# One head's keys and values side by side: a regrouped pooling product in a fused attention, Fourier and feed-forward kernel

## The chip, the cores and the metric

The kernel runs on one core of a Trainium2 chip, in one launch. The metric is the device time of that launch in microseconds (us). A core has five engines that work side by side and hand over to each other by semaphores: TensorE (PE) multiplies matrices, VectorE (DVE), ScalarE (ACT) and GpSimd (POOL) do elementwise work, and SyncE (SP) issues the DMAs. PE takes a stationary matrix (a weight load, shown as PEld) and streams moving columns through it.

## The reference

For each of 8 batches and 8 heads, 576 tokens are pooled to 32 memory slots, and then every token attends to those slots. The result goes through a two-dimensional Fourier transform whose real part is added, a normalisation, and a feed-forward layer with a residual.

```python
a = exp(phi - max(phi));  a = a / (sum(a) + 1e-9)        # 576 x 32 per head
k_m = einsum('bhsm,bhsd->bhmd', a, k)                    # pooled keys,   32 x 64
v_m = einsum('bhsm,bhsd->bhmd', a, v)                    # pooled values, 32 x 64
attn = softmax(q @ k_m.T / sqrt(64));  x = attn @ v_m
u = x + real(fft(fft(x, axis=1), axis=2))
un = (u - mean(u)) / sqrt(var(u) + 1e-6)
out = u + relu(un @ w1) @ w2                             # 512 -> 2048 -> 512
```

## The kernel before, in words

Single-precision values are carried as two 16-bit parts, a high one and a low one, so that a product of two of them is three matmuls: high by high, low by high, high by low (low by low is dropped). The tokens of the feed-forward layer are cut into 18 chunks of 256. Each chunk goes through 8 units: in `ffn1_sums` 24 matmuls of 256 columns build a hidden tile `ph`, which ACT (L944) and DVE (L945) move out of PSUM as a high and a low part; in `ffn2` 12 matmuls of 512 columns accumulate into `po`. These two are most of what PE does.

The attention is written as a generator, `background()`, and the unit loop draws one step of it per unit. A scheduler that works at build time then interleaves everything and fixes the order on every engine; on the chip each engine runs its list in that order, and waits where an operand is not there yet.

The change is in `pair_memory`, for the batches from the third on (`b >= NX`, `NX = 2`): six batches of four pairs of heads, so 24 calls. A pair's keys and values arrive in one tile `kv` of 5 token tiles by 2 (`w` = 0 for keys, 1 for values) by 128 columns (two heads of 64). They are squared for a scale (L474, and L477 for the queries), scaled and cut into parts: the high part by ACT (L488), the low part of the keys by DVE (L495), the low part of the values by an ACT copy (L490) and a POOL subtraction (L491), because `KP = [1]`. The parts lie in `kvs`, the pooling weights of two pairs in `et`, also as high and low.

The pooling itself is two groups of 15 matmuls, first keys, then values, each of 64 moving columns (the 32 slots of both heads):

```python
for ka, kb in ((0, 0), (1, 0), (0, 1)):
    for t in range(NST):
        mm(pm[:, w * 64 : w * 64 + 64], lhsT=kvs[ka][:, t, w, :],
           rhs=et[:, g // 2, kb, t, 64 * (g % 2) : 64 * (g % 2) + 64], ...)
```

Half of what comes out, one head's keys with the other head's weights, is not wanted; the mask `mk` takes it away when DVE reads the keys (L516) and the values (L517) out of PSUM. The keys are then cut into parts (`km`, L526 on ACT and L527 on DVE) for `pair_scores`, whose 18 matmuls `psc` follow. At the end of a batch `values` multiplies the pooled values by a constant matrix that `load_vt` brings in (`pv`, L695), and `mix_x` uses them once more (`px`).

Of the kernel before, what the change touches and what calls it, by code (L numbers as in the profile page):

```python
# [10 lines left out]
F32 = mybir.dt.float32  # L11
F16 = mybir.dt.float16
BF16 = mybir.dt.bfloat16
# [3 lines left out]
AF = mybir.ActivationFunctionType  # L17
ALU = mybir.AluOpType
AX = mybir.AxisListType
PSUM = bass.MemoryType.PSUM  # L20

P = 128
B, H, S, D, M = 8, 8, 576, 64, 32
# [6 lines left out]
NST = 5  # L30
# [19 lines left out]
GATE2 = [[], ["un1", "qs0"]] + [["un1", f"ev{j - 2}"] for j in range(2, 8)]  # L50
NA = 2
NAH = 1
KP = [1]
BN = 2
UB = 2
NW = NF // UB
# [1 line left out]
EB = 14  # L58
# [80 lines left out]
def kernel(  # L139
# [10 lines left out]
    nc = tc.nc  # L150

    const = ctx.enter_context(tc.tile_pool(name="const", bufs=1))
# [9 lines left out]
    et = const.tile([P, 2, 2, NST, P], F16, name="et")  # L162
# [11 lines left out]
    small = const.tile([P, 832], F32, name="small")  # L174
    mk = small[:, 0:68]
    ones = small[:, 68:132].bitcast(BF16)
    qsb = [small[:, 196 + i * 258 : 196 + i * 258 + NJ] for i in range(2)]
    half = small[:, 712:713]
    drop = small[:, 715:716]
# [11 lines left out]
    stg = const.tile([P, 3, 4 * UW], F16, name="stg")  # L191
# [6 lines left out]
    hring = const.tile([P, NW, 2, 4, P], F16, name="hring")  # L198

    nk = 2 * NST * P  # L200
    kvs = [stg[:, 2, i * nk : (i + 1) * nk].rearrange("p (t w c) -> p t w c", t=NST, w=2) for i in range(2)]
    qs = [stg[:, 2, 2 * nk + i * NQ : 2 * nk + (i + 1) * NQ] for i in range(2)]
    et32 = et.rearrange("p g l t c -> p (g l t c)").bitcast(F32).rearrange("p (g t c) -> p g t c", g=2, t=NST)

# [28 lines left out]
    vmc = vmf.rearrange("p g u c -> p (g u c)")[:, : H * M]  # L233
# [2 lines left out]
    nc.gpsimd.memset(drop, 2.0**-14 - 0.5)  # L236
    for t in qsb:
        nc.gpsimd.memset(t, 0.0)
    scratch = const.tile([P, 400], F32, name="scratch")
    share = const.tile([P, 2 * NJ], F32, name="share")  # L240
    rings, taken = {}, [0]

    def tiny(tag, n, bufs=2):
        if tag not in rings:
            rings[tag] = [taken[0], 0]
            taken[0] += n * bufs
        o, i = rings[tag]
        rings[tag][1] += 1
        o += i % bufs * n
        assert taken[0] <= 400, taken  # L250
        return scratch[:, o : o + n]

    def high_words(t):
# [84 lines left out]
    def load_vt():  # L338

        v = stg[:, 1] if marks.get("vt") else hring.rearrange("p a l f c -> p (a l f c)")[:, : NG * 2 * DM]  # L340
        marks["vt"] = nc.sync.dma_start(out=v, in_=vt_d)
        return [v[:, g * 2 * DM : (g + 1) * 2 * DM] for g in range(NG)]

    def pooling_f32(b):
# [94 lines left out]
    def pair_memory(b, g, r, vmf, ivs):  # L439

        n = f"{b}_{g}"
        kv = r[:, :KV].rearrange("p (t w c) -> p t w c", t=NST, w=2)
        q = r[:, KV:]
        if b < NX:
            pm = psg.tile([P, 512], F32, tag="g", name=f"pm_{n}")
            mm = groups()
            busy = keep_busy(0, 0, f"pm_{n}") if b == 0 else None
            for w in range(2):
                for t in range(NST):
                    m = mm(  # L450
                        pm[:, w * 64 : w * 64 + 64],
                        lhsT=kv[:, t, w, :],
                        rhs=et32[:, g // 2, t, 64 * (g % 2) : 64 * (g % 2) + 64],
                        start=(t == 0),
                        stop=(t == NST - 1),
                    )
                    if b == 0:
                        keep_busy(1, 2 * P, n, busy, m)
            if b == 0 and g == 1:
                keep_busy(10, 2 * P, n, busy, m)  # L460
            kmf = share[:, g * 64 : g * 64 + 64] if b == 0 else tiny("kmf", 64, 2)
            mask = share[:, 256 + g * 64 : 320 + g * 64] if b == 0 else mk[:, 0:64]
            marks["kmf"] = marks[f"kmf{n}"] = nc.vector.tensor_tensor(out=kmf, in0=pm[:, 0:64], in1=mask, op=ALU.mult)
            nc.vector.tensor_tensor(
                out=vmf[:, g],
                in0=pm[:, 64:128].unsqueeze(1).to_broadcast([P, 2, 64]),
                in1=mask.unsqueeze(1).to_broadcast([P, 2, 64]),
                op=ALU.mult,
            )
            return q, None, kmf, 1.0 / 8.0  # L470
        am = tiny("am", 3, 1)
        with tc.issue_after(marks["wh3"].ins) if b == NX and g == 0 else nullcontext():
            for w in range(2):
                nc.scalar.activation(  # L474
                    kvs[0][:, :, w, :].bitcast(BF16), kv[:, :, w, :], AF.Square, accum_out=am[:, 1 + w : 2 + w]
                )
            nc.scalar.activation(  # L477
                kvs[1][:, 0:3].rearrange("p t w c -> p (t w c)").bitcast(BF16), q, AF.Square, accum_out=am[:, 0:1]
            )
        pm = psg.tile([P, 512], F32, tag="g", name=f"pm_{n}")  # L480
        mm = groups()
        mm(pm[:, 128:131], lhsT=ones, rhs=high_words(am), start=True, stop=True)
        sc = tiny("sc", 3, 2)
        isc = tiny("isc", 3, 2)
        norm_scale(sc, isc, pm[:, 128:131], 3, 14, n)
        nc.vector.tensor_copy(out=ivs[:, g : g + 1], in_=isc[:, 2:3])
        for w in range(2):
            nc.scalar.activation(kvs[0][:, :, w, :], kv[:, :, w, :], AF.Copy, scale=sc[:, 1 + w : 2 + w])  # L488
            if w in KP:
                nc.scalar.activation(kv[:, :, w, :], kv[:, :, w, :], AF.Copy, scale=sc[:, 1 + w : 2 + w])  # L490
                nc.gpsimd.tensor_tensor(  # L491
                    out=kvs[1][:, :, w, :], in0=kv[:, :, w, :], in1=kvs[0][:, :, w, :], op=ALU.subtract
                )
            else:
                nc.vector.scalar_tensor_tensor(  # L495
                    out=kvs[1][:, :, w, :],
                    in0=kv[:, :, w, :],
                    scalar=sc[:, 1 + w : 2 + w],
                    in1=kvs[0][:, :, w, :],
                    op0=ALU.mult,  # L500
                    op1=ALU.subtract,
                )
        for w in range(2):
            i = 0
            for ka, kb in ((0, 0), (1, 0), (0, 1)):
                for t in range(NST):
                    mm(
                        pm[:, w * 64 : w * 64 + 64],
                        lhsT=kvs[ka][:, t, w, :],
                        rhs=et[:, g // 2, kb, t, 64 * (g % 2) : 64 * (g % 2) + 64],  # L510
                        start=(i == 0),
                        stop=(i == 3 * NST - 1),
                    )
                    i += 1
        kmf = tiny("kmf", 64, 2)
        nc.vector.tensor_tensor(out=kmf, in0=pm[:, 0:64], in1=mk[:, 0:64], op=ALU.mult)  # L516
        nc.vector.scalar_tensor_tensor(  # L517
            out=vmc[:, g * 64 : g * 64 + 64],
            in0=pm[:, 64:128],
            scalar=isc[:, 2:3],  # L520
            in1=mk[:, 0:64],
            op0=ALU.mult,
            op1=ALU.mult,
        )
        km = tiny("km", 64).bitcast(F16).rearrange("p (l c) -> p l c", l=2)
        nc.scalar.copy(out=km[:, 0], in_=kmf)  # L526
        nc.vector.tensor_tensor(out=km[:, 1], in0=kmf, in1=km[:, 0], op=ALU.subtract)  # L527
        es = tiny("es", 1, 2)
        nc.vector.tensor_scalar(
            out=es, in0=isc[:, 0:1], scalar1=isc[:, 1:2], scalar2=1.0 / 8.0, op0=ALU.mult, op1=ALU.mult  # L530
        )
        return q, sc, km, es
# [215 lines left out]
    def mix_x(b, key, col, n, rows, attnT, vbd):  # L748
        px = psg.tile([P, 512], F32, tag="g", name=f"px_{b}_{key}")
        mm = groups()  # L750
        if b >= NX:
            for h in range(H):
                o = 64 * (h % 2)
                mm(
                    px[rows, h * 64 : h * 64 + 64],
                    lhsT=stack[h // 2][:, col // P * 2 + h % 2, col % P : col % P + n],
                    rhs=vbd[:, h, o : o + 64],
                    start=True,
                    stop=True,
                )  # L760
            return px
        vbd = vbd.rearrange("p (l g) f -> p l g f", l=2)
        for g in range(NG):
            for l in range(2):
                marks["px"] = mm(
                    px[rows, g * P : (g + 1) * P],
                    lhsT=attnT[:, g, col // P, col % P : col % P + n],
                    rhs=vbd[:, l, g, :],
                    start=(l == 0),
                    stop=(l == 1),  # L770
                )
        return px
# [457 lines left out]
    marks = {}  # L1230
# [106 lines left out]

    load_phi(0)
    nc.scalar.dma_start(out=mk, in_=mk_d)
    nc.scalar.activation(warm, warm, AF.Exp)  # L1340
    keep_busy(14, 2 * P, "start")
    parts_w1, parts_w2 = {}, {}
# [182 lines left out]
```

## Time and profile before

| | us |
|---|---|
| three runs | 938.22, 940.21, 937.79 |
| median | 938.22 |
| profiled execution, span from first to last instruction | 935.8 |
| PE busy | 925.7 (99%) |
| DVE busy | 635.4 (68%) |
| ACT busy | 498.2 (53%) |
| POOL busy | 222.3 (24%) |

The profile gives the span of the profiled execution; the time of a run holds also what lies around the span. A row of the lists by line reads: line, engine, operation, output <- inputs, shape, count, then the busy time in us and the mean length of one in ns, then the idle time of the engine just ahead of it. The lengths of matmuls overlap, since they are pipelined, so a run of them in the timeline, with its start, its length and its count, tells more than the mean. In the timeline a bracket at the end names an idle time before the row and what ended it.

### The profile page before, as it was taken

Reading aid. Unit: us, or ns where it says so; the run is one execution under the profiler, and the core shown is the slowest. Engines: PE = TensorE matmul, PEld = TensorE weight load, DVE = VectorE, ACT = ScalarE, POOL = GpSimd, SP = SyncE. Lnnn points to the kernel's source line nnn. Section 1 sums busy time; section 2 is a strip of 40 time slices with the busy share of each in tenths; the row PEclk is TensorE's granted clock in tenths of the full one; section 3 lists DMA queues with packets and bytes.
Section 4 is the critical chain, followed back from the end, with each engine's and each line's share of the span. In section 5 each row is a group of like instructions: output and inputs, shape, how many; then the busy total and the mean of one; then the engine's idle time right before and its main releaser. Section 6 shows DMA issues by size and latency. Waiting matters only on the chain.

```text
span 935.8 us, 19497 instructions
## 1 busy us (share of the span) xinstructions
PE 925.7 (99%) x7982; PEld 682.6 (73%) x7982; DVE 635.4 (68%) x1406; ACT 498.2 (53%) x980; POOL 222.3 (24%) x248
## 2 busy tenths in 40 slices
PE   8999999999999999999999999999999999999998
PEld 8776776667767677777767767777676777788886
DVE  4899786777677766667414876667555686985454
ACT  4678557765376536554414654655445543643331
POOL 3310142424133313323100331324120422100000
PEclk9999999999999999999999999999999999999999
DMA  9964651365246522844103541274215311202000
GB/s 353 368 233 135 206 143 14 83 146 118 50 88 141 118 49 56 169 88 108 22 25 69 142 115 49 38 191 108 38 46 97 97 27 37 46 23 47 1 23 23
DMA packets 131321, 92.04 MB, mean 98 GB/s; under 512 B 115744, under 2 KB 115744, under 8 KB 129184
## 3 DMA queue, kind: packets, MB, share of 16 engines
q1 hardware_dynamic: 131088, 90.77, 38.1%
q8 instruction: 62, 1.02, 0.5%
q14 instruction: 27, 0.22, 0.1%
q10 hardware_dynamic: 144, 0.03, 0.0%
HBM read 58.15 MB, written 9.44 MB: 72 GB/s over the span
## 4 chain that ended last, share of the span: by engine, by line
PE 82%; DVE 9%; ACT 4%; POOL 2%; issue 1%; DMA 0%; SPq 0%; DVEq 0%; ACTq 0%; POOLq 0%
PE ph L315 34%; PE po L954 29%; PE pm L315 3%; PE po L1044 3%; PE pq L1044 3%; PE psc L315 2%; PE pp_t L315 2%; PE po L913 1%; PE ph L891 1%; PE pa L726 1%; PE pv L695 1%; PE px_t L315 1%; DVE uring L825 1%; DVE w1t L1194 1%; DVE un L852 1%
## 5 line engine op out<-in xcount | busy, mean ns | idle before, releaser
L315 PE MATMUL ph<-unring,w1t 128*128 128x256 f16 x3264 | 388.8, 273 | 0.0
L315 PEld LDWEIGHTS <-w1t 128*128 128x128 f16 x3324 | 318.9, 98 | 58.4 <-issue 1.6
L954 PE MATMUL po<-w2s,hring 128*128 128x512 f16 x1368 | 319.8, 379 | 0.0
L954 PEld LDWEIGHTS <-hring 128*128 128x128 f16 x1368 | 130.8, 98 | 129.9 <-issue 0.5
L945 DVE SCALAR_TENSOR_TENSOR hring<-ph,hring 128x512 f16<-128x512 f32 x114 | 78.1, 685 | 52.4 <-ACT hring L944 51.9
L944 ACT ACTIVATE hring<-ph 128x512 f16<-128x512 f32 x114 | 67.0, 588 | 61.8 <-PE ph L315 61.3
L613 POOL TENSOR_TENSOR aring<-aring,scratch 128x384 f32<-128x384 f32 x30 | 26.8, 894 | 242.8 <-DVE scratch L611 197.3
L851 POOL TENSOR_TENSOR scratch<-scratch,small 128x1 f32<-128x1 f32 x36 | 22.4, 627 | 164.6 <-DVE scratch L848 160.8
L315 PEld LDWEIGHTS <-stg 128*128 128x128 f16 x1152 | 45.0, 98 | 10.7 <-issue 1.5
L550 ACT CAST aeo<-eo 128x384 f16<-128x384 f32 x30 | 15.3, 510 | 51.3 <-DVE eo L547 51.3
L605 ACT ACTIVATE aring<-aring,scratch 128x384 f32<-128x384 f32 x24 | 14.6, 609 | 46.9 <-DVE aring L602 46.9
L543 DVE TENSOR_TENSOR eo<-aring 128x128 f32<-128x128 f32 x29 | 35.4, 1221 | 4.9 <-POOL aring L630 4.9
L315 PE MATMUL pm<-et,stg 128*128 128x64 f16 (+1 forms) x780 | 37.0, 199 | 0.4 <-DMA et<-elt 0.4
L811 DVE SCALAR_TENSOR_TENSOR share<-pp_t,scratch,small 128x257 f32<-128x257 f32 (+1 forms) x48 | 21.1, 481 | 23.8 <-ACT small L807 22.4
L593 DVE TENSOR_REDUCE scratch<-psc 128x12 f32<-128x384 f32 x32 | 17.7, 554 | 27.7 <-PE pm L315 16.7
L630 POOL TENSOR_TENSOR aring<-aring 128x128 f32<-128x128 f32 x60 | 35.3, 608 | 2.3
L877 POOL TENSOR_TENSOR ud<-un,ud 128x1024 f16<-128x1024 f32 x13 | 27.6, 2126 | 30.8 <-ACT ud L876 30.8
L825 DVE SCALAR_TENSOR_TENSOR uring<-px_t,scratch,share 128x256 f32<-128x256 f32 (+1 forms) x80 | 34.2, 478 | 0.3 <-PE px_t L315 0.2
L491 POOL TENSOR_TENSOR stg<-rawt,stg 128x640 f16<-128x640 f32 x12 | 17.2, 1431 | 72.6 <-ACT rawt L490 72.6
L625 POOL TENSOR_TENSOR hring<-aring,hring 128x640 f16<-128x640 f32 x24 | 34.1, 1421 | 0.1
L1008 ACT ACTIVATE rawt<-ph 128x512 f32<-128x512 f32 x22 | 13.1, 596 | 35.0 <-PE ph L315 35.0
L891 PE MATMUL ph<-unring,w1t 128*128 128x256 f32 (+1 forms) x144 | 30.2, 358 | 0.7 <-ACT unring L863 0.7
(321 smaller groups left out, 1530.5 us busy)
## 6 DMA issues: line engine op xcount, KB each, us to landing
rawt<-in_raw SPq DMA_DIRECT2D x15, 640.0 KB, 4.8
stg<-in_raw SPq DMA_DIRECT2D x15, 640.0 KB, 5.3
out<-uring SPq DMA_DIRECT2D x36, 256.0 KB, 2.1
stg<-in_w SPq DMA_DIRECT2D x7, 1024.0 KB, 5.9
rawt<-in_raw SPq DMA_DIRECT2D x15, 384.0 KB, 3.3
stg<-in_raw SPq DMA_DIRECT2D x15, 384.0 KB, 3.1
phs<-in_raw SPq DMA_DIRECT2D x32, 160.0 KB, 5.3
w2s<-in_w SPq DMA_DIRECT2D x4, 1024.0 KB, 9.2
```

Of the source, the lines that this page charges most:

```text
L315: m = nc.tensor.matmul(out, lhsT=lhsT, rhs=rhs, start=start, stop=stop)
L543: nc.vector.tensor_tensor(out=eo[:, 0, 1:3], in0=ap[:, 1:3, 0], in1=ap[:, 1:3, 1], op=ALU.add)
L613: eng.tensor_tensor(out=a, in0=a, in1=sm.unsqueeze(2).to_broadcast([P, 12, M]), op=ALU.mult)
L625: nc.gpsimd.tensor_tensor(out=ahw[:, :, :, 1], in0=a10, in1=ahw[:, :, :, 0], op=ALU.subtract)
L630: eng.tensor_tensor(out=a2[:, i : i + 4], in0=a[:, 0:4], in1=a[:, 4:8], op=op)
L825: nc.vector.scalar_tensor_tensor(out=u[rows, hs], in0=px[rows, hs], scalar=igx[rows], in1=tm[rows, w * NJ + half : w * NJ + half + 256], o ...
L877: marks[f"ul{c}"] = (nc.vector if c in (1, LC, LC + 1, LC + 2) else nc.gpsimd).tensor_tensor(out=ud[:, 1], in0=un, in1=ud[:, 0], op=ALU.su ...
L891: marks[f"f1_{j}"] = nc.tensor.matmul(ph[:, cols], lhsT=w[:, k, f * P : (f + 1) * P], rhs=unTs[0][:, k, cols], start=(k == 0), stop=(k == ...
L944: marks[f"ev{c}_{j}"] = nc.scalar.activation(h[:, 0], phv, AF.Relu)
L945: nc.vector.scalar_tensor_tensor(out=h[:, 1], in0=phv, scalar=0.0, in1=h[:, 0], op0=ALU.max, op1=ALU.subtract)
L954: m = nc.tensor.matmul(po[t], lhsT=hs[j][:, lh, f * 2 + t], rhs=w2s[:, j * UB + f, lw, :], start=(j == 0 and f == 0 and i == 0), stop=(j = ...
L1044: m = nc.tensor.matmul(dst[:, half_n * 256 : half_n * 256 + 256], lhsT=a[:, la, f], rhs=b[:, f, lb], start=begin, stop=False, skip_group_c ...
```

## The change

Keys and values change places in the stationary matrix: instead of the keys of both heads, then the values of both heads, a matrix now holds one head's keys and the same head's values (64 + 64 columns). The moving columns are that head's 32 high weights and its 32 low weights together. So per head 5 matmuls of 64 columns do high by high and high by low at once, and 5 of 32 columns add low by high onto the first half; 20 matmuls in place of 30. The two halves of the result are then added by a new DVE reduction, and the keys and values are taken out of that sum (in SBUF, no longer in PSUM) with `mk` and its complement `mkv`, a new small tile that one POOL instruction makes near the start.

Two things follow from the layout. For the second head the columns stand as values, keys, so `parts_of` gives the keys the quarters 0 and 3 and the values 1 and 2; and the pooled values land on the other half of the partitions than before, so the second load of `load_vt` is done as two DMAs with the halves exchanged, and `mix_x` takes the other column offset. The parts of keys and values also exchange engines (`KP = [0]`): the low part of the keys is now made by ACT and POOL, that of the values by DVE.

```diff
-KP = [1]
+KP = [0]
...
-        marks["vt"] = nc.sync.dma_start(out=v, in_=vt_d)
+        halves = [slice(0, 64), slice(64, P)]
+        for dst, src in zip(halves, halves[::-1]) if marks.get("vt") else ((slice(0, P), slice(0, P)),):
+            load = nc.sync.dma_start(out=v[dst], in_=vt_d[src])
+        marks["vt"] = load
...
-            nc.scalar.activation(kvs[0][:, :, w, :], kv[:, :, w, :], AF.Copy, scale=sc[:, 1 + w : 2 + w])
+            src = kv[:, :, w, :].rearrange("p t (h c) -> p t h c", h=2)
+            hi, lo = (k[:, :, parts_of[w]] for k in kvs)
+            nc.scalar.activation(hi, src, AF.Copy, scale=sc[:, 1 + w : 2 + w])
...
-        for w in range(2):
-            i = 0
-            for ka, kb in ((0, 0), (1, 0), (0, 1)):
+        for h in range(2):
+            c0 = 64 * (g % 2) + 32 * h
+            heads = [k[:, :, 2 * h : 2 * h + 2].rearrange("p t x c -> p t (x c)") for k in kvs]
+            for t in range(NST):
+                both = mm(
+                    pm[:, h * 64 : h * 64 + 64],
+                    lhsT=heads[0][:, t],
+                    rhs=et[:, g // 2, :, t, c0 : c0 + M],
+                    start=(t == 0),
+                    stop=(t == NST - 1),
+                )
+            with tc.issue_after(both.ins):
                 for t in range(NST):
-                    mm(
-                        pm[:, w * 64 : w * 64 + 64],
...
+                    nc.tensor.matmul(
+                        pm[:, h * 64 : h * 64 + M],
+                        lhsT=heads[1][:, t],
+                        rhs=et[:, g // 2, 0, t, c0 : c0 + M],
+                        start=False,
...
-        kmf = tiny("kmf", 64, 2)
-        nc.vector.tensor_tensor(out=kmf, in0=pm[:, 0:64], in1=mk[:, 0:64], op=ALU.mult)
+        kmf, kvm = tiny("kmf", 64, 2), tiny("kvm", 64, 1)
+        nc.vector.tensor_reduce(
+            out=kvm.rearrange("p (h m) -> p h m", h=2),
+            in_=pm[:, 0:128].rearrange("p (h l m) -> p h m l", h=2, l=2),
+            axis=AX.X,
+            op=ALU.add,
+        )
+        nc.vector.tensor_tensor(out=kmf, in0=kvm, in1=mk[:, 0:64], op=ALU.mult)
...
+            out=vmc[:, g * 64 : g * 64 + 64], in0=kvm, scalar=isc[:, 2:3], in1=mkv, op0=ALU.mult, op1=ALU.mult
...
-                o = 64 * (h % 2)
+                o = 64 * (1 - h % 2)
...
+    nc.gpsimd.tensor_scalar(out=mkv, in0=mk[:, 0:64], scalar1=-1.0, scalar2=2.0**-EB, op0=ALU.mult, op1=ALU.add)
```

Since the scheduler runs again, the order moves as well, from the third batch on. The places below are the third pair of the fourth batch. The changed kernel's lines are numbered differently: L957, L498, L500, L479, L485 and L539 are L944, L488, L490, L474, L477 and L526 of before.

On PE, in the kernel before, this is where that pair's last ten `pm` matmuls stand, between the units `ph_6`:

```order
L315 LDWEIGHTS w1t
L315 MATMUL ph_6_3547<-unring,w1t 128x256
L315 LDWEIGHTS stg
L315 MATMUL pm_2_3409<-et,stg 128x64
L315 LDWEIGHTS stg
```

And this is the changed kernel's, the place where the first head's low part (32 columns) ends and the second head's 64 columns begin:

```order
L519 LDWEIGHTS stg
L519 MATMUL pm_2_3357<-et,stg 128x32
L317 LDWEIGHTS stg
L317 MATMUL pm_2_3357<-et,stg 128x64
L317 LDWEIGHTS stg
```

Before, the groups of a pair were mostly 20 and 10 (or 5, 15 and 10); now they are 5 (the first head's high part) and 15, and all that needs a low part is in the 15.

On ACT, before, the same pair, from the high parts (L488, keys and values) to the copy that POOL waits for (L490) and the next pair's squares (L474, L477):

```order
L488 ACTIVATE stg<-rawt,scratch 128x5x128 x2
L578 ACTIVATE stg<-rawt,scratch 128x768
L490 ACTIVATE rawt<-rawt,scratch 128x5x128
L624 CAST hring<-aring 128x20x32
L474 ACTIVATE stg,scratch<-stg 128x5x128
L550 CAST aeo<-eo 128x6x64
L944 ACTIVATE hring<-ph_5_3467 128x512
L477 ACTIVATE stg,scratch<-stg 128x768
L474 ACTIVATE stg,scratch<-stg 128x5x128
L526 CAST scratch<-scratch 128x64
```

And the changed kernel's:

```order
L498 ACTIVATE stg<-rawt,scratch 128x5x2x64
L498 ACTIVATE stg<-rawt,scratch 128x5x128
L591 ACTIVATE stg<-rawt,scratch 128x768
L957 ACTIVATE hring<-ph_6_3486 128x512
L500 ACTIVATE rawt<-rawt,scratch 128x5x128
L637 CAST hring<-aring 128x20x32
L563 CAST aeo<-eo 128x6x64
L479 ACTIVATE stg,scratch<-stg 128x5x128
L957 ACTIVATE hring<-ph_7_3565 128x512
L479 ACTIVATE stg,scratch<-stg 128x5x128
L485 ACTIVATE stg,scratch<-stg 128x768
L539 CAST scratch<-scratch 128x64
```

The work is the same; one eviction of `ph` now stands ahead of the copy for POOL, and the cast to `aeo` ahead of the first square.

On DVE, before, what follows the pair's last `pm` matmul:

```order
L945 SCALAR_TENSOR_TENSOR hring<-ph_5_3467,hring 128x512
L516 TENSOR_TENSOR scratch<-pm_2_3409,small 128x64
L517 SCALAR_TENSOR_TENSOR vmf<-pm_2_3409,scratch,small 128x64
L527 TENSOR_TENSOR scratch<-scratch 128x64
L945 SCALAR_TENSOR_TENSOR hring<-ph_6_3547,hring 128x512
```

And now:

```order
L958 SCALAR_TENSOR_TENSOR hring<-ph_7_3565,hring 128x512
L528 TENSOR_REDUCE scratch<-pm_2_3357 128x64
L534 TENSOR_TENSOR scratch<-scratch,small 128x64
L535 SCALAR_TENSOR_TENSOR vmf<-scratch,small 128x64
L540 TENSOR_TENSOR scratch<-scratch 128x64
L958 SCALAR_TENSOR_TENSOR hring<-ph_0_3643,hring 128x512
```

The reduction is new, and the keys' product (L534) and the values' (L535) stand behind it, between the same two evictions.

## Rows read from the trace of the kernel before

**Rows 1.** The page: engines, and the granted TensorE clock in 40 slices.

```profile
PE 925.7 (99%) x7982; PEld 682.6 (73%) x7982; DVE 635.4 (68%) x1406; ACT 498.2 (53%) x980; POOL 222.3 (24%) x248
...
PEclk9999999999999999999999999999999999999999
```

**Rows 2.** Windows: stretch, length, then busy us of PE, PEld, DVE, ACT, POOL.

```profile
100.00:130.00 30.00, 30.00 (x197) 24.56 (x196) 22.21 (x50) 14.52 (x28) 10.28 (x16) 1.00 0.65 199
...
275.00:331.00 56.00, 56.00 (x542) 39.04 (x541) 40.16 (x89) 32.57 (x67) 18.54 (x20) 1.00 0.62 135
```

**Rows 3.** Timeline, one pair of the fourth batch: start, length, engine, line, count.

```profile
300.96 1.91 PE L315 MATMUL ph<-unring,w1t 128*128 128x256 f16 x16
...
302.71 0.31 PE L315 MATMUL pm<-et,stg 128*128 128x64 f16 x5
...
302.96 0.60 PE L315 MATMUL pm<-et,stg 128*128 128x64 f16 x15
...
303.86 1.40 POOL L491 TENSOR_TENSOR stg<-rawt,stg 128x640 f16<-128x640 f32 x1
...
307.34 0.59 ACT L944 ACTIVATE hring<-ph 128x512 f16<-128x512 f32 x1
...
307.74 0.46 PE L315 MATMUL pm<-et,stg 128*128 128x64 f16 x10
...
308.25 0.68 DVE L945 SCALAR_TENSOR_TENSOR hring<-ph,hring 128x512 f16<-128x512 f32 x1
...
308.85 0.21 DVE L516 TENSOR_TENSOR scratch<-pm,small 128x64 f32<-128x64 f32 x1
...
309.67 2.75 PE L954 MATMUL po<-w2s,hring 128*128 128x512 f16 x12
...
309.90 0.23 DVE L527 TENSOR_TENSOR scratch<-scratch 128x64 f16<-128x64 f32 x1 [0.65 <-ACT scratch L526]
...
312.26 0.93 PE L315 MATMUL ph<-unring,w1t 128*128 128x256 f16 x7
313.02 0.70 PE L315 MATMUL psc<-scratch,stg 128*128 128x64 f16 x18
313.56 0.17 PE L315 MATMUL pm<-scratch,small 128*128 128x3 bf16 x1
313.59 0.60 PE L315 MATMUL ph<-unring,w1t 128*128 128x256 f16 x4
```

**Rows 4.** Timeline of PE: other runs of narrow matmuls.

```profile
159.22 0.61 PE L315 MATMUL px_t<-vbdt,attnT 128*128 128x128 f16 x8
...
160.98 1.06 PE L315 MATMUL px_t<-vbdt,attnT 128*128 128x128 f16 x16
...
184.45 1.03 PE L315 MATMUL pm<-et,stg 128*128 128x64 f16 x30 [0.40 <-DMA et<-elt]
...
204.82 0.22 PE L315 MATMUL psc<-scratch,stg 128*128 128x64 f16 x2 [0.38 <-ACT scratch L526]
```

**Rows 5.** Lists by line and shape, whole span: a reduction out of PSUM.

```profile
L593 DVE TENSOR_REDUCE scratch<-psc 128x12 f32<-128x384 f32 x32 | 17.7, 554 | 27.7 <-PE pm L315 16.7 <-PE psc L315 10.8
```

**Rows 6.** Timeline of POOL near the start, and one small reduction on DVE.

```profile
19.65 1.60 POOL L613 TENSOR_TENSOR aring<-aring,scratch 128x384 f32<-128x384 f32 x1 [15.11 <-DVE scratch L611]
...
22.16 0.80 POOL L628 TENSOR_TENSOR ahring<-aring,ahring 128x320 f16<-128x320 f32 x1
...
168.68 0.28 DVE L416 TENSOR_REDUCE scratch<-pl 128x2 f32<-128x128 f32 x1
```

**Rows 7.** A DMA's size and us to landing; SP's issues; their use on PE.

```profile
stg<-in_vt SPq DMA_DIRECT2D x1, 1024.0 KB, 4.8
...
107.61 0.33 SPq L335 DMA_DIRECT2D stg<-in_raw  x1
...
115.05 0.33 SPq L335 DMA_DIRECT2D stg<-in_raw  x1
...
122.32 2.40 PE L315 MATMUL pm<-et,stg 128*128 128x64 f32 x20
```

More of the change, by code (lines that the diff above doesn't have):

```diff
@@ L176 @@
     ones = small[:, 68:132].bitcast(BF16)
+    mkv = small[:, 132:196]
     qsb = [small[:, 196 + i * 258 : 196 + i * 258 + NJ] for i in range(2)]
@@ L200 @@
     nk = 2 * NST * P
-    kvs = [stg[:, 2, i * nk : (i + 1) * nk].rearrange("p (t w c) -> p t w c", t=NST, w=2) for i in range(2)]
+    kvs = [stg[:, 2, i * nk : (i + 1) * nk].rearrange("p (t x c) -> p t x c", t=NST, x=4) for i in range(2)]
+    parts_of = (slice(0, 4, 3), slice(1, 3))
     qs = [stg[:, 2, 2 * nk + i * NQ : 2 * nk + (i + 1) * NQ] for i in range(2)]
@@ L238 @@
         nc.gpsimd.memset(t, 0.0)
-    scratch = const.tile([P, 400], F32, name="scratch")
+    scratch = const.tile([P, 464], F32, name="scratch")
     share = const.tile([P, 2 * NJ], F32, name="share")
@@ L249, in tiny @@
         o += i % bufs * n
-        assert taken[0] <= 400, taken
+        assert taken[0] <= 464, taken
         return scratch[:, o : o + n]
@@ L474, in pair_memory @@
                 nc.scalar.activation(
-                    kvs[0][:, :, w, :].bitcast(BF16), kv[:, :, w, :], AF.Square, accum_out=am[:, 1 + w : 2 + w]
+                    kvs[0][:, :, 2 * w : 2 * w + 2].rearrange("p t x c -> p t (x c)").bitcast(BF16),
+                    kv[:, :, w, :],
+                    AF.Square,
+                    accum_out=am[:, 1 + w : 2 + w],
                 )
             nc.scalar.activation(
-                kvs[1][:, 0:3].rearrange("p t w c -> p (t w c)").bitcast(BF16), q, AF.Square, accum_out=am[:, 0:1]
+                kvs[1][:, 0:3].rearrange("p t x c -> p (t x c)").bitcast(BF16), q, AF.Square, accum_out=am[:, 0:1]
             )
@@ L487, in pair_memory @@
         for w in range(2):
-            nc.scalar.activation(kvs[0][:, :, w, :], kv[:, :, w, :], AF.Copy, scale=sc[:, 1 + w : 2 + w])
+            src = kv[:, :, w, :].rearrange("p t (h c) -> p t h c", h=2)
+            hi, lo = (k[:, :, parts_of[w]] for k in kvs)
+            nc.scalar.activation(hi, src, AF.Copy, scale=sc[:, 1 + w : 2 + w])
             if w in KP:
[L490 to L493, printed above, removed]
+                nc.scalar.activation(src, src, AF.Copy, scale=sc[:, 1 + w : 2 + w])
+                nc.gpsimd.tensor_tensor(out=lo, in0=src, in1=hi, op=ALU.subtract)
@@ L494, in pair_memory @@
             else:
                 nc.vector.scalar_tensor_tensor(
[L496 to L501, printed above, removed]
-                )
-        for w in range(2):
-            i = 0
-            for ka, kb in ((0, 0), (1, 0), (0, 1)):
-                for t in range(NST):
-                    mm(
-                        pm[:, w * 64 : w * 64 + 64],
[L509 to L512, printed above, removed]
-                    )
-                    i += 1
@@ L515, in pair_memory @@
-        kmf = tiny("kmf", 64, 2)
-        nc.vector.tensor_tensor(out=kmf, in0=pm[:, 0:64], in1=mk[:, 0:64], op=ALU.mult)
-        nc.vector.scalar_tensor_tensor(
[L518 to L523, printed above, removed]
+                    out=lo, in0=src, scalar=sc[:, 1 + w : 2 + w], in1=hi, op0=ALU.mult, op1=ALU.subtract
+                )
+        for h in range(2):
[10 more added lines that the diff above has]
+            with tc.issue_after(both.ins):
+                for t in range(NST):
+                    nc.tensor.matmul(
[3 more added lines that the diff above has]
+                        start=False,
+                        stop=(t == NST - 1),
+                        skip_group_check=True,
+                    )
```

## The prediction

> **What bounds the kernel now.** I read the page first: PE is busy for 99% of the span, and the granted clock is at its upper level, 2.4 GHz, in every slice [rows 1]. The clock therefore has nothing to give or to take in the stretch where the change lies. A busy share made of pipelined, overlapping matmuls proves little, so the second view was the windows: over the fourth batch PE is busy 56.00 of 56.00 us, while DVE has 40.16, ACT 32.57 and POOL 18.54 [rows 2]. The third view was the timeline of one pair, read by the starts of the runs and not by their lengths. The 12 `po` matmuls at 309.67 are followed by `ph` at 312.26, which is 2.59 us or 0.216 each; the 7 `ph` by `psc` at 313.02, 0.109 each; the 18 `psc` by the next at 313.56, 0.030 each; the 16 `ph` at 300.96 by `pm` at 302.71, again 0.109 each [rows 3]. Every run starts when the count of the one before it, at a fixed price per matmul, is used up. So PE's list is packed there: what is taken out of it should come off the end, as long as the other engines keep up.
>
> The Trainium skill warns here ("Trainium Kernel Development and Optimization", Performance Expectations) that matmul busy time is a poor measure, because matmuls are pipelined; taken alone, the 99% could hide idle time, and then removing matmuls would save nothing. The starts above are what decides it, and they show no such idle time.
>
> **The change part by part.** *The matmuls taken out.* 24 calls lose 10 of 30 matmuls each, with their weight loads. Their price is the step from one to the next: 30 take 1.03 us [rows 4] and 5 take 0.31 [rows 3], so 25 more cost 0.72, which is 0.0288 us each. The weight load is inside that, since it runs beside the matmul ahead. 24 x 10 x 0.0288 = 6.9 us, all on PE.
>
> *The matmuls made narrower.* Ten of the remaining 20 stream 32 columns and not 64. No row shows 32. From below: the product with 3 columns at 313.56 is followed after 0.03 us [rows 3], at a resolution of 0.01, which is no less than 64 columns cost; then nothing is gained. From above: 128 columns cost (1.06 - 0.61) / 8 = 0.056 us [rows 4], so 64 columns fewer save 0.0275; in proportion, 32 fewer would save 0.0137, and 240 of them 3.3 us. I stay near the row with the fewest columns and take 0.026 us, an estimate, so 240 x 0.003 = 0.7 us.
>
> The Trainium skill has a rule on this which speaks against half of the idea ("TensorE: Matmul & The Clock Gate", the section "Wait — 56ns, not 53.3ns?"): however few columns, the step from one matmul to the next stays at about 25 ns, and it gives that figure for 32 columns. By it the term would be an estimated 240 x 0.0038 = 0.9 us; in proportion to the columns it would be 3.3. The row with 3 columns goes with the rule.
>
> *The new reduction on DVE.* 24 of them, 128 elements in, 64 out, out of PSUM. The nearest rows are a reduction of 128 elements at 0.28 us [rows 6] and one of 384 at 0.554 [rows 5]; I take 0.3. DVE's other two instructions keep their shapes and read SBUF; I take them at what they cost now. On DVE's time that is 24 x 0.3 = 7.2 us, beside PE: in the fourth batch 1.2 us more on an engine that idles 16 of 56 [rows 2]. In the chain it lengthens the way from the last `pm` to `psc`. That way has room: the last `pm` run ends at 308.20, the low part of the keys (L527) is done at 310.13, and PE comes to `psc` at 313.02, 2.9 us later [rows 3]. In the changed order the distance between the two on PE is not shorter in this pair. If that cover were gone, the 7.2 us would come onto the end.
>
> *Keys and values exchange engines.* The counts of ACT, DVE and POOL instructions for the parts stay. The group of 15 that now ends a pair needs the POOL subtraction, as the group of 10 did. Before, POOL is done at 303.86 + 1.40 = 305.26 and the group starts at 307.74, 2.5 us later [rows 3]. In the new order one eviction (0.59 us) stands ahead of the ACT copy that POOL waits for, so I count 1.9 us of room. POOL now reads and writes in pieces of 64: at 0.80 us for 320 elements in such pieces [rows 6] against 1.40 for 640 it would take at most 1.6, so 0.2 of the 1.9. Cost nothing; bounds 0 and, if the room is gone in every pair, the lateness itself.
>
> *Waits that may go.* In the third batch PE waits 0.38 us for ACT ahead of a `psc` [rows 4]; there the new order puts a larger distance between `pm` and `psc`. The 0.40 for a DMA [rows 4] stands where the order is unchanged and stays. I count 0.4 us gained, between 0 and 0.8.
>
> *The second `load_vt` in halves.* One more DMA issue on SP (0.33 us), and the half loads may use the rings less well: at worst each takes the 4.8 us of the whole [rows 7], so what is queued behind comes 4.8 + 0.3 us later. Behind stand a pair's loads, issued at 107.61 (keys and values) and 115.05 (queries); PE uses the first from 122.32 on, the queries later still [rows 7]. Issued 5.1 us later and landing within 4.8 us, the time of the larger DMA, the first would be there at 117.5, and PE's order there is unchanged. Cost nothing; without the cover at most 5 us, once. The matrix itself is first used in the third batch.
>
> *The new tile `mkv`.* One POOL instruction near the start, where POOL idles 15.11 us [rows 6]. Nothing.
>
> **The sum.** 6.9 + 0.7 + 0.4 = 8.0 us off PE's list. The span of the profiled execution, 935.8, becomes 927.8; the median of the runs shown is 938.22, 2.4 us more, which I take as what lies around the span and leave alone: 930.2 us. The own range of this forecast is 6.9 + 0 + 0 less about 1 for waits at new places, up to 6.9 + 2 + 0.8: 928.5 to 932.3.
>
> **Rivals.** *A larger gain, 927.6 us.* If the narrow matmuls cost in proportion to their columns, the sum is 6.9 + 3.3 + 0.4 = 10.6. For it: between 64 and 128 columns the price does go with the columns. Against: the row with 3 columns.
>
> *The gain is waited away, about 938 us.* The group of 15 needs the low parts of keys and values at once, and stands ahead of everything PE does next. It starts to cost when POOL comes more than 1.9 us later than I count, for instance because ACT stands longer at a cast that waits for DVE, which now has more to do. To bring the result inside what a measurement can tell, 5.2 of the 8.0 us must go, 0.22 in each of 24 pairs. For it: the 0.38 us wait shows that such a place can be cut too fine. Against: that is one place, and 2.5 us is what the pair in the rows has in hand.
>
> *Slower, about 945 us.* The mechanism is the eviction of `ph`. The reduction and the two products stand on DVE between two evictions, and PE has two `ph` buffers only. In the rows, one buffer is evicted by ACT at 307.34 and freed by DVE at 308.25 + 0.68 = 308.93, and PE writes it again at 312.26, 3.3 us later [rows 3]. From 3.3 us of added delay on, each further bit is PE's. To end slower than before by more than can be told, the 8.0 and 2.8 more must be lost, 0.45 us per pair, so 3.8 us of delay in each; with 0.6 us per pair the time is 938.2 - 8.0 + 24 x 0.6 = 944.6. Against: the added DVE work is 0.3 us a pair, a tenth of it.
>
> **How the numbers follow.** About 0.3% (2.8 us) is what a measurement of this kernel can tell from no change. The forecast has 0.72, the larger gain 0.13, the gain waited away 0.10, slower 0.05. Faster is the sum of the first two, 0.85; the same 0.10; slower 0.05. The range goes down to 926.5, which takes in the larger gain and a little more, and up to 935.5, which takes in waits that eat two thirds of the gain; what it leaves out is the two last cases.
>
> **What would show it.** In the profile after: PE with 480 instructions fewer, half of them matmuls; steps of 0.029 us in `pm` runs of 64 columns and of about 0.026 in those of 32, to be read from the starts; DVE with 24 reductions of about 0.3 us; PE still without idle time in the fourth batch; no wait of `pm` on POOL and none of `ph` on DVE. It would be wrong if PE's named waits grow by several us, if the 32-column runs step by 0.015 or by more than 0.03, or if the span falls by less than PE's list has become shorter.

## The result and the profile after

The changed kernel takes 931.07 us (median of 4 runs, 930.39 to 931.12) against 938.57 (median of 4, 937.79 to 940.21) for the kernel before: a ratio of 0.9917, 95% interval 0.9903 to 0.9931. The forecast was 930.2, range 926.5 to 935.5. The span of the profiled execution went from 935.8 to 928.9 us.

The page of the changed kernel, in its part on the engines and the clock, stands against [rows 1]:

```profile
span 928.9 us, 19062 instructions
...
PE 917.7 (99%) x7742; PEld 674.6 (73%) x7742; DVE 641.8 (69%) x1430; ACT 497.2 (54%) x980; POOL 233.5 (25%) x249
...
PEclk9999999999999999999999999999999999999999
```

PE has 240 matmuls and 240 weight loads fewer and is busy for 8.0 us less; the clock is the same. DVE has its 24 reductions more and 6.4 us more to do, and POOL, with one instruction more, 11.2 us more. The last number was not foreseen; 10 of the 11.2 lie in the subtraction of the parts (L501, below, against 24 times 1.40 [rows 3]).

The timeline of PE in the third pair of the fourth batch answers to [rows 3]. The columns are start, length, engine, line, output and inputs, shape and count:

```profile
310.38 0.31 PE L317 MATMUL pm<-et,stg 128*128 128x64 f16 x5
310.53 1.36 PE L317 MATMUL ph<-unring,w1t 128*128 128x256 f16 x11
311.73 2.75 PE L967 MATMUL po<-w2s,hring 128*128 128x512 f16 x12
314.32 0.27 PE L317 MATMUL ph<-unring,w1t 128*128 128x256 f16 x1
314.43 0.28 PE L519 MATMUL pm<-et,stg 128*128 128x32 f16 x5
314.56 0.31 PE L317 MATMUL pm<-et,stg 128*128 128x64 f16 x5
314.70 0.28 PE L519 MATMUL pm<-et,stg 128*128 128x32 f16 x5
314.83 1.36 PE L317 MATMUL ph<-unring,w1t 128*128 128x256 f16 x11
```

Read by the starts, five matmuls of 32 columns take 0.13 us (314.43 to 314.56, and 314.70 to 314.83), 0.026 each, and five of 64 columns 0.14 to 0.15, 0.029 each. A pair's 20 cost 0.55 us, where 30 cost 0.86 to 0.87. The runs again follow each other without a gap.

The lists by line and shape show the new and the exchanged instructions. Of each row the count, the busy time and the mean length in ns matter:

```profile
L501 POOL TENSOR_TENSOR stg<-stg 128x640 f16<-128x640 f32 x12 | 22.6, 1884 | 20.1 <-ACT stg L500 19.5
L501 POOL TENSOR_TENSOR stg<-rawt,stg 128x640 f16<-128x640 f32 x12 | 21.0, 1752 | 59.4 <-ACT rawt L500 58.9
...
L503 DVE SCALAR_TENSOR_TENSOR stg<-stg,scratch 128x640 f16<-128x640 f32 x12 | 14.1, 1176 | 3.8 <-ACT stg L498 3.7
...
L528 DVE TENSOR_REDUCE scratch<-pm 128x64 f32<-128x128 f32 x24 | 6.8, 284 | 2.9 <-PE pm L519 2.9
```

The reduction is 0.284 us, near the 0.3 taken. The POOL subtraction, 1.40 us before [rows 3], is now 1.75 to 1.88 on the mean of its two rows.

The list of PE's waits (who waited for whom, us in total, times, longest) has one entry over 0.2 us that the kernel before did not have, `ph` for DVE:

```profile
PE ph L317 <- DVE hring L958: 1.4, 2, 0.7
PE psc L317 <- DVE share L468: 1.0, 2, 0.8
```

The wait of `psc` for ACT [rows 4] is gone, and `ph` waits twice for DVE. One of the two, in the timeline of PE, DVE and ACT at the end of the fourth batch:

```profile
328.17 1.55 DVE L560 TENSOR_TENSOR eo<-aring 128x192 f32<-128x192 f32 x1
...
329.75 0.51 ACT L563 CAST aeo<-eo 128x384 f16<-128x384 f32 x1 [3.09 <-DVE eo L560]
330.17 0.73 ACT L479 ACTIVATE stg<-rawt 128x640 bf16<-128x640 f32 x1
...
330.90 0.57 ACT L957 ACTIVATE hring<-ph 128x512 f16<-128x512 f32 x1
331.02 0.59 PE L967 MATMUL po<-w2s,hring 128*128 128x512 f16 x2
...
331.50 0.69 DVE L958 SCALAR_TENSOR_TENSOR hring<-ph,hring 128x512 f16<-128x512 f32 x1 [0.34 <-ACT hring L957]
...
332.25 2.78 PE L317 MATMUL ph<-unring,w1t 128*128 128x256 f16 x24 [0.63 <-DVE hring L958]
```

ACT stands for 3.09 us at a cast that needs the result of DVE's L560. Behind the cast stand a square and the eviction of `ph` (330.90), then DVE's half of the eviction ends at 332.19, and PE, which is ready for the next `ph` about 331.6, starts it at 332.25. So PE stands 0.63 us in the fourth batch, where it had stood not at all [rows 2].

### The profile page after: what moved, and what is told of

It reads as the page before. It is cut to its first block, busy times and chain, and to the rows that moved or that the text cites. A ratio compares the mean times of both kernels' runs of the same rounds, so it can differ in the third digit from the quotient of the medians.

```text
span 928.9 us, 19062 instructions
## 1 busy us (share of the span) xinstructions
PE 917.7 (99%) x7742; PEld 674.6 (73%) x7742; DVE 641.8 (69%) x1430; ACT 497.2 (54%) x980; POOL 233.5 (25%) x249
## 4 chain that ended last, share of the span: by engine, by line
PE 82%; DVE 10%; ACT 4%; POOL 2%; issue 2%; DMA 1%; SPq 0%; DVEq 0%; POOLq 0%; ACTq 0%
PE ph L317 35%; PE po L967 29%; PE po L1057 3%; PE pq L1057 3%; PE psc L317 2%; PE pm L317 2%; PE pp_t L317 2%; PE po L926 1%; PE ph L904 1%; PE pa L739 1%; PE pv L708 1%; PE px_t L317 1%; DVE uring L838 1%; DVE w1t L1207 1%; PE pm L519 1%
## 5 line engine op out<-in xcount | busy, mean ns | idle before, releaser
L957 ACT ACTIVATE hring<-ph 128x512 f16<-128x512 f32 x114 | 66.8, 586 | 59.5 <-PE ph L317 59.4
L501 POOL TENSOR_TENSOR stg<-rawt,stg 128x640 f16<-128x640 f32 x12 | 21.0, 1752 | 59.4 <-ACT rawt L500 58.9
L556 DVE TENSOR_TENSOR eo<-aring 128x128 f32<-128x128 f32 x29 | 29.5, 1017 | 3.8 <-POOL aring L643 3.8
L317 PEld LDWEIGHTS <-stg 128*128 128x128 f16 x672 | 28.2, 97 | 4.6 <-issue 0.9
L926 PE MATMUL po<-w2s,hring 128*128 128x512 f32 x64 | 29.7, 599 | 0.2 <-ACT hring L912 0.2
```

What stands on the lines that cost most here:

```text
L317: m = nc.tensor.matmul(out, lhsT=lhsT, rhs=rhs, start=start, stop=stop)
L556: nc.vector.tensor_tensor(out=eo[:, 0, 1:3], in0=ap[:, 1:3, 0], in1=ap[:, 1:3, 1], op=ALU.add)
L926: marks[f"f2_{j}"] = nc.tensor.matmul(po[t], lhsT=h[:, f, t], rhs=w[:, f], start=(j == 0 and f == 0), stop=(j == NW - 1 and f == UB - 1),)
L957: marks[f"ev{c}_{j}"] = nc.scalar.activation(h[:, 0], phv, AF.Relu)
```

## The experiments

Each was timed in five rounds beside the kernel before; a time is a median, a ratio is that to the kernel before with its 95% interval.

**High and low weights merged, the stationary matrix left alone.** This takes the count of matmuls apart from the columns.

```diff
-            for ka, kb in ((0, 0), (1, 0), (0, 1)):
...
+            for t in range(NST):
+                both = mm(pm[:, w * 128 : w * 128 + 128], lhsT=kvs[0][:, t, w, :],
+                    rhs=et[:, g // 2, :, t, c0 : c0 + 64], start=(t == 0), stop=(t == NST - 1))
...
+                    nc.tensor.matmul(pm[:, w * 128 : w * 128 + 64], lhsT=kvs[1][:, t, w, :],
+                        rhs=et[:, g // 2, 0, t, c0 : c0 + 64], start=False, ...)
```

> The kernel before, with high and low weights side by side as 128 moving columns and the stationary matrix left as it was (keys of two heads, values of two heads): 20 matmuls a pair in place of 30, but the same 1920 columns, and a DVE reduction. My theory (a step costs its columns: 0.056 us for 128, 0.029 for 64) expects 10 x 0.056 + 10 x 0.029 = 0.85 us a pair against 0.86, so no gain from PE, 938 to 939.5 us, ratio 0.999 to 1.001. The rival (each matmul with its weight load has a fixed price, so the count decides) expects the 6.9 us of the changed kernel, 931.7 us, ratio 0.993.

Measured: 938.72 us, ratio 1.0011 (1.0002 to 1.0019). 240 matmuls fewer and nothing gained. The timeline of PE shows where they went:

```profile
278.44 0.44 PE L315 MATMUL pm<-et,stg 128*128 128x128 f16 x5
278.72 0.31 PE L515 MATMUL pm<-et,stg 128*128 128x64 f16 x5
278.86 0.44 PE L315 MATMUL pm<-et,stg 128*128 128x128 f16 x5
279.14 0.31 PE L515 MATMUL pm<-et,stg 128*128 128x64 f16 x5
279.29 2.57 PE L315 MATMUL ph<-unring,w1t 128*128 128x256 f16 x22
```

From 278.44 to 279.29 is 0.85 us, as expected, where 30 matmuls of 64 columns cost 0.86. A wait of 1.45 us of `psc` for ACT in the third batch, in place of the 0.38 [rows 4], is of the size of the 0.9 us that the version loses. So the count is not what pays: the changed kernel gains because its regrouped stationary matrix no longer streams one head's weights through another head's columns, 960 columns a pair in place of 1920.

**The low by high matmuls widened to 64 columns.**

```diff
-                        pm[:, h * 64 : h * 64 + M],
+                        pm[:, h * 64 : h * 64 + 64],
...
-                        rhs=et[:, g // 2, 0, t, c0 : c0 + M],
+                        rhs=et[:, g // 2, :, t, c0 : c0 + M],
```

> The changed kernel, with the low by high matmuls widened from 32 to 64 moving columns (high and low weights both, which adds the low by low product). 24 x 10 = 240 matmuls change. My theory (a step costs about the same at 32 columns as at 64: 0.026 against 0.029 us) expects +0.8 us over the changed kernel, 931.9 us, ratio to before 0.9925. The rival (the price goes with the columns) expects +3.3 us, 934.4 us, ratio 0.9956.

Measured: 932.25 us, ratio 0.9938 (0.9926 to 0.9950). That is 1.2 us above the changed kernel's 931.07, nearer the 0.8 of the one theory than the 3.3 of the other. But the two were timed in different sessions and the intervals overlap: by the ratios the distance is 2.0 us, and against the changed kernel's repeat below (931.95) it is 0.3. The times alone do not decide; the steps do. In the timeline of PE the four runs of a pair now start evenly:

```profile
281.08 0.31 PE L317 MATMUL pm<-et,stg 128*128 128x64 f16 x5
281.23 0.31 PE L519 MATMUL pm<-et,stg 128*128 128x64 f16 x5
281.37 0.31 PE L317 MATMUL pm<-et,stg 128*128 128x64 f16 x5
281.52 0.31 PE L519 MATMUL pm<-et,stg 128*128 128x64 f16 x5
```

0.14 to 0.15 us for five, against 0.13 with 32 columns. Halving these columns gave the forecast's 0.003 us each.

**The high matmuls done twice.**

```diff
+            for t in range(NST):
+                both = mm(pm[:, 256 + h * 64 : 256 + h * 64 + 64], lhsT=heads[0][:, t],
+                    rhs=et[:, g // 2, :, t, c0 : c0 + M], start=(t == 0), stop=(t == NST - 1))
```

> The changed kernel with each head's 5 high matmuls of 64 columns done a second time, into columns of the PSUM tile that nothing reads: 240 matmuls with their weight loads more. My theory (PE's list is packed, each step of 64 columns costs 0.0288 us wherever it stands) expects +6.9 us over the changed kernel, 937.5 to 938.5 us, ratio 0.999 to 1.0005. The rival (part of such steps falls into time in which PE waits anyway) expects less than +5 us, under 936 us, ratio under 0.998.

The version serves for its time alone. Measured: 936.92 us, ratio 0.9990 (0.9981 to 0.9999): 5.9 us above the changed kernel, 6.2 by the spans (935.1 against 928.9), 6.8 by the ratios and 5.0 against the repeat below. This lies between the two theories. The order differs, and with it the waits: the 1.4 us of `ph` for DVE are gone, and shorter ones came. The list of PE's waits:

```profile
PE psc L317 <- DVE scratch L548: 0.6, 1, 0.6
...
PE px_t L317 <- DMA hring<-hring: 0.4, 1, 0.4
PE pm L527 <- POOL stg L501: 0.3, 1, 0.3
```

Most of a step in PE's list comes through to the end. It can be told to about a microsecond, since each rebuild places some waits anew and the sessions differ.

**The exchange of engines alone, in the kernel before.**

```diff
-KP = [1]
+KP = [0]
```

> The kernel before with the exchange of engines alone: keys' low part by ACT and POOL, values' by DVE. PE's list keeps all its matmuls. My theory expects no gain: 938.5 to 940 us, ratio 1.000 to 1.0015, with waits of PE of up to 1.5 us more. The rival (the exchange brings part of the gain) expects 936 us or less, ratio under 0.9975.

Measured: 941.23 us, ratio 1.0036 (1.0023 to 1.0049), 3.4 us slower than the 937.85 beside it. The rival falls, and the loss is larger than I expected. It lies at one place in the last batch, in the timeline of PE and DVE and, in the last row, by the windows (as in [rows 2]; the third number from the end is the granted share of PE's clock):

```profile
719.76 0.22 PE L315 MATMUL psc<-scratch,stg 128*128 128x64 f16 x2
...
721.87 0.69 DVE L979 TENSOR_TENSOR elt<-phs 128x512 f32<-128x512 f32 x1 [6.26 <-DMA et<-elt]
...
722.75 0.64 PE L315 MATMUL psc<-scratch,stg 128*128 128x64 f16 x16 [2.77 <-DVE scratch L527]
...
723.25 2.45 PE L315 MATMUL ph<-unring,w1t 128*128 128x256 f16 x12
...
723.00:726.00 3.00, 3.00 (x28) 2.13 (x25) 2.41 (x9) 0.88 (x2) 0.00 (x0) 0.59 0.00 0
```

PE waits 2.77 us for L527, the low part of the pooled keys. In DVE's list L527 stands behind L979, which waits 6.26 us for a DMA and belongs to the weights of the last chunks, not to the parts of keys and values. After PE's standstill the granted clock is 0.59 on the mean from 723 to 726, where it is 1.00 from 720 to 723: for most of that stretch PE ran at its lower level, 1.2 GHz. The 12 `ph` matmuls take 2.24 us to the next run at 725.49; 12 at 0.109 would have taken 1.31. The wait and these 0.9 us are more than the 3.4 us lost. In the kernel before the same two DVE instructions stand in the same order, but the DMA is done earlier:

```profile
719.27 0.69 DVE L979 TENSOR_TENSOR elt<-phs 128x512 f32<-128x512 f32 x1 [4.38 <-DMA et<-elt]
...
719.93 0.86 PE L315 MATMUL psc<-scratch,stg 128*128 128x64 f16 x18
```

The same `psc` starts at 719.93 there and at 719.76 here, so up to this place the exchange had cost nothing.

The lists by line of the same run show the parts' POOL subtractions, in pieces of 128 columns as before the change:

```profile
L491 POOL TENSOR_TENSOR stg<-stg 128x640 f16<-128x640 f32 x12 | 23.9, 1988 | 14.7 <-ACT stg L490 7.6 <-issue 6.3
L491 POOL TENSOR_TENSOR stg<-rawt,stg 128x640 f16<-128x640 f32 x12 | 20.3, 1691 | 57.3 <-ACT rawt L490 56.8
```

The POOL subtraction is 1.69 to 1.99 us here too, so its length comes with the exchange and not with the pieces of 64; the last section shows how.

**The exchange undone in the changed kernel.** The keys' quarters lie apart, so DVE needs two instructions for them.

```diff
-KP = [0]
+KP = [1]
...
+            elif w == 0:
+                for h in range(2):
+                    nc.vector.scalar_tensor_tensor(out=lo[:, :, h], in0=src[:, :, h],
+                        scalar=sc[:, 1 + w : 2 + w], in1=hi[:, :, h], op0=ALU.mult, op1=ALU.subtract)
```

> The changed kernel with the exchange of engines undone: the low part of the keys on DVE (in two instructions, one for each head, since their quarters lie apart), that of the values by ACT and POOL. My theory (the gain is PE's shorter list, and the exchange gives 1 to 2 us back through late evictions) expects PE's two waits on DVE, 1.4 us in the profile, to be gone and 929.5 to 931 us, ratio 0.990 to 0.992. The rival (the exchange brings part of the gain) expects a slower kernel, 933 us or more, ratio 0.994 or more.

Measured: 929.03 us, ratio 0.9903 (0.9891 to 0.9916), a little under what I expected. Its list of PE's waits has no `ph` on DVE, and a wait of `pm` for a DMA that is longer than before the change (0.4 [rows 4]):

```profile
PE psc L317 <- DVE share L468: 1.1, 2, 0.8
PE pm L317 <- DMA et<-elt: 1.0, 2, 0.5
```

At the place of the wait shown above, the timeline of PE and DVE has:

```profile
331.12 0.93 PE L317 MATMUL ph<-unring,w1t 128*128 128x256 f16 x7
...
332.48 0.69 DVE L968 SCALAR_TENSOR_TENSOR hring<-ph,hring 128x512 f16<-128x512 f32 x1 [0.35 <-ACT hring L967]
```

The eviction ends at 333.17, not earlier than the 332.19 of the changed kernel. But here PE starts its `ph` 2 us before that end, and there only after it.

The subtraction is short again, by the list of lines:

```profile
L501 POOL TENSOR_TENSOR stg<-rawt,stg 128x640 f16<-128x640 f32 x12 | 18.6, 1548 | 40.9 <-ACT rawt L500 40.9
L501 POOL TENSOR_TENSOR stg<-stg 128x640 f16<-128x640 f32 x12 | 16.7, 1393 | 0.0
```

To see it beside the changed kernel on one chip, both were run once more.

> The changed kernel once more, unaltered, beside the next one on the same chip. Both theories expect 930.4 to 931.3 us, ratio 0.9917.

> The changed kernel with the exchange of engines undone (the low part of the keys on DVE in two instructions, that of the values by ACT and POOL), once more, beside the changed kernel on the same chip. My theory (the exchange gives back 1 to 2 us through two late evictions, which is no chance of one chip) expects 1.2 to 2.2 us less than the changed kernel beside it, and both waits of ph on DVE gone again. The rival (the difference between the runs lay between the chips) expects the two within 0.6 us of each other.

Measured: the changed kernel 931.95 us (ratio 0.9939, 0.9925 to 0.9952), the version with the exchange undone 928.84 (0.9905, 0.9891 to 0.9918), so 3.1 us less by the medians, more than the 1.2 to 2.2 expected, and 1.5 by the spans of the profiled executions (928.3 and 926.8). The changed kernel's repeat is itself above the 930.4 to 931.3 that I expected and 5.8 us under the kernel before beside it, where the first measurement had 7.5: what the change gains is known to about 2 us. In the first, the two waits of `ph` on DVE are there with 1.4 us; in the second they are not. The difference is not one of chips, and this version beats both kernels.

**Both low parts on DVE.** As the last edit, with `KP = []`.

> The changed kernel with both low parts on DVE (three instructions a pair), so the ACT copies (24 of 0.82 us) and the POOL subtractions go and DVE gets some 24 us more. My theory (the evictions come late because ACT stands behind casts that wait for DVE and POOL; with POOL out of the pair they come earlier, as long as DVE has room) expects 928.5 to 930.5 us, ratio 0.989 to 0.9915. The rival (DVE has no such room in the attention's stretches) expects waits of PE on DVE of 4 us and more and 933 us or more.

Measured: 930.20 us, ratio 0.9920 (0.9907 to 0.9933). The time is in the expected range. `ph` still waits for DVE, 1.1 us in two waits, but at other places, by the timeline of PE:

```profile
604.84 2.78 PE L317 MATMUL ph<-unring,w1t 128*128 128x256 f16 x24 [0.72 <-DVE hring L968]
...
645.11 2.78 PE L317 MATMUL ph<-unring,w1t 128*128 128x256 f16 x24 [0.33 <-DVE hring L968]
```

The changed kernel's stand at 332.25 and 542.27. So such waits come without any subtraction of the parts on POOL, and a rebuild moves them; that POOL's longer subtraction causes the two of the changed kernel is neither shown nor ruled out.

**Without the reduction.**

```diff
-        nc.vector.tensor_reduce(
...
+        kvm = pm[:, 0:128].rearrange("p (h l m) -> p h l m", h=2, l=2)[:, :, 0]
```

> The changed kernel without the new DVE reduction: keys and values are taken from the first half of the product alone, so the high by low term is left out of the result. DVE has 24 instructions, 6.8 us, less. My theory (the reduction lies beside PE) expects the time of the changed kernel within 1 us, 930 to 931.5 us, ratio 0.991 to 0.993. The rival (the reduction lengthens the chain to the scores and costs what it takes) expects 924 to 926 us, ratio 0.985 to 0.988.

Measured: 930.57 us, ratio 0.9920 (0.9907 to 0.9934), the changed kernel's time within 0.5 us. The 6.8 us of reductions lie beside PE, as far as a rebuild can tell: its PE list has a new wait of 0.8 us of `psc` for DVE, so a microsecond of cost could hide behind it, not 6.8.

**The second load in halves, in the kernel before.**

```diff
+        for part in (slice(0, 64), slice(64, P)) if marks.get("vt") else (slice(0, P),):
+            load = nc.sync.dma_start(out=v[part], in_=vt_d[part])
...
```

> The kernel before with the second load of the constant matrix as two DMAs of 64 partitions each, not exchanged, and nothing else. My theory (covered: the loads behind have room) expects no change, 937.5 to 938.5 us, ratio 0.9995 to 1.0005. The rival (the loads behind come late and PE waits for them once) expects up to +5 us, ratio up to 1.005, with a wait of pm or psc on a DMA of in_raw near 115 to 130 us in the profile.

Measured: 937.76 us against 937.83, ratio 0.9997 (0.9988 to 1.0005). No change. The list of DMA issues gives the halves' landing time, 6.4 us each against 4.8 for the whole [rows 7]:

```profile
stg<-in_vt SPq DMA_DIRECT2D x2, 512.0 KB, 6.4
```

## Why the prediction was right, and where it was not

- *What bounds the kernel.* Right. PE's list is packed; work taken off DVE (the reduction) moved nothing that can be told, and 240 matmuls put back cost 5.0 to 6.8 us, by the run they are set against, where their steps come to 6.9.
- *The matmuls taken out, 6.9 us.* Right in size. The words put it as a price for each matmul with its weight load; the merged kernel shows that the price is that of 64 columns, not of an instruction.
- *The matmuls made narrower, 0.7 us.* Right: 0.026 us a step by the trace, which makes 240 x 0.003. The rival with the larger gain falls by the same step. The Trainium skill's figure of 25 ns for 32 columns ("TensorE: Matmul & The Clock Gate", the section "Wait — 56ns, not 53.3ns?") agrees with the trace to 0.001 us.
- *The reduction, nothing.* Right: 0.284 us, and no difference without it that can be told.
- *Waits that may go, 0.4 us.* Half right. That wait went, and two others came, 1.4 us by name, so this term is about 1 us to the other side: 6.9 + 0.7 - 1.0 = 6.6, where the spans show 6.9.
- *Keys and values exchange engines, nothing.* This term was mis-sized. The version with the exchange undone is faster than the changed kernel beside it by 1.5 us (spans) to 3.1 (medians), and of this the two waits of the term above are the 1.4 us that have a name. In the kernel before, the exchange cost 3.4 us, but by a DMA wait in DVE's list and the clock after it, at one place. I bounded the POOL subtraction by the pieces of 64 at 1.6 us; it became 1.75 to 1.88, and for another reason, since it is as long with pieces of 128.
- *What would show it.* Most of it did, but `ph` waited for DVE, so that PE stood 0.63 us in the fourth batch. And one sign of being wrong came: the span fell by 6.9 us where PE's list became 7.6 shorter by its steps. Both come from the same miss, that of the waits.
- *The slower rival.* Its mechanism, PE held by an eviction of `ph`, is real, but at 2 places in all and not in each of 24 pairs, and 0.7 us each.
- *The load in halves.* Right in that it costs nothing, but its bound was wrong: the halves landed in 6.4 us each, not within the 4.8 of the whole.

That the forecast came within 0.9 us of the result is in part luck. The waits were off by 1.4 us, which alone would have made 931.6. Against that, the span fell by 0.3 us more than the named terms make up, and what lies around the span was 2.2 us where I took 2.4. What stays open is why `ph` waits in the changed kernel. The cast ahead of the eviction waits for DVE's L560, which runs beside POOL, and POOL's longer subtraction comes just before; but with the exchange undone the eviction is no earlier, and PE does not wait for it. Whether the longer instructions or the other order is the cause was not separated.

## What to carry to other kernels

Where PE is packed, count the columns that it streams, not the instructions: putting two operands side by side gains nothing by itself, and a stationary matrix that holds only what belongs to the same moving columns gains part of the masked half, here 0.31 of 0.86 us a pair. It is not the whole half, because below 64 columns the step hardly shrinks. When a layout forces an exchange between engines, time the exchange by itself and look at where the loss falls: a single wait that the rebuilt order makes, and the slower clock after it, can cost as much as half of the gain.

## What was not expected of the hardware

The POOL subtraction of 640 elements took 1.39 us at its shortest and up to 2.22 in the changed kernel, and DVE's instructions vary in the same way with what POOL does. In the kernel before, DVE takes longer beside the same subtraction [rows 3], by the timeline:

```profile
303.94 1.48 DVE L543 TENSOR_TENSOR eo<-aring 128x128 f32<-128x128 f32 x1 [0.36 <-POOL aring L630]
```

In the changed kernel DVE is still at the low part of the queries (L592) when the subtraction begins. The same DVE instruction as above is now L556; the last row is one with no POOL instruction beside it:

```profile
309.20 1.22 DVE L592 SCALAR_TENSOR_TENSOR stg<-rawt,scratch,stg 128x768 f16<-128x768 f32 x1
309.71 1.98 POOL L501 TENSOR_TENSOR stg<-rawt,stg 128x640 f16<-128x640 f32 x1
...
310.95 0.88 DVE L556 TENSOR_TENSOR eo<-aring 128x128 f32<-128x128 f32 x1
...
771.29 0.28 DVE L556 TENSOR_TENSOR eo<-aring 128x128 f32<-128x128 f32 x1
```

That instruction needs 0.28 us and was held back in both kernels: it ends some 0.15 us after the subtraction does, at 305.42 after 305.26 before, and at 311.83 after 311.69 now. The subtraction in turn ends some 1.26 us after the L592 beside which it began (310.42), nearly the length that it has alone. In the changed kernel 19 of the 24 subtractions begin beside an L592, and all 19 end 1.25 to 1.26 us after it; in the kernel before only 4 of 24 begin so. This is why the subtraction became longer: the one that comes second stands until the other is done. The Trainium skill ("SBUF — State Buffer", the section "Who interferes with whom") says that a VectorE instruction with two inputs in SBUF contends with a GpSimd instruction that reads SBUF, over a pair of ports that is locked for one of them. These rows agree: all of these instructions read two tiles, or two parts of one, in SBUF.
